# Giving 64 rows of one weight matrix to three of sixteen DMA engines, and moving a small scaling from VectorE to ScalarE

## The chip, the cores and the metric

One core of one Trainium2 chip. The metric is the device time of one launch in microseconds; the kernel before takes 526.28 us (median of three runs, 526.14 to 526.68). The span is the time from the first to the last instruction of a profiled run.

## The reference

One decode step of a transformer block: layer norm of x (4 x 640), attention of 32 heads over a cached window, and a gated feed-forward network, all added up.

```python
xn = layernorm(x)                                   # B=4, D=640
q  = (xn @ wq) ...                                  # 32 heads of 192
k, v = k_cache[:, :, -2048:], v_cache[:, :, -2048:] # 2 x 32 heads x 3 MB, bf16
o  = softmax(q k^T * 192**-0.5) v @ wo
h  = silu(xn @ w1) * (xn @ w3)                      # w1, w3: 640 x 1536
out = x + o + h @ w2                                # w2: 1536 x 640
```

Everything except x is read exactly once, 223 MB in all, and there are only four rows to multiply it with. The kernel is a stream of loads with some arithmetic beside it.

## The kernel before

All large loads are issued by SyncE in one order, and each is split over the 16 DMA engines of the core. K has two buffers, V three, the feed-forward weights one. The program is a list of slots; `add(slot, phase, fn)` puts a step into it.

```python
def load_k(h):
    kt = kpool.tile([P, NJ, Dh], BF16, tag="kt")                      # 2 buffers
    nc.sync.dma_start(out=kt[:]..., in_=k_win[:, h].rearrange("b (p j) d -> p b (j d)", p=PB))
...
xn = const.tile([B, D], BF16, name="xn")
nc.vector.tensor_scalar_mul(out=xn[:], in0=xc[:], scalar1=rstd[:, 0:1])   # line 194
...
def mult(u):                      # VectorE; the last quarter of a head frees its K buffer
    nc.vector.tensor_tensor(out=pr[:], in0=kts[h][:, g * JQ:(g + 1) * JQ, :], in1=qbc[...], op=ALU.mult)
...
def chain_gmax(h):
    ...
    nc.vector.tensor_scalar_mul(out=gneg[:], in0=gmax[:]..., scalar1=-SCALE)   # the softmax shift
...
def ffn_load(name, w, *at):       # w1 in two transfers, w3 in three, over all 128 partitions
    wt = fpool.tile([P, KC, F], BF16, tag="w", name=name)
    for k0, k1 in zip((0,) + at, at + (KC,)):
        nc.sync.dma_start(out=wt[:, k0:k1, :]..., in_=w.rearrange("(p kc) n -> p kc n", kc=KC)[:, k0:k1, :]...)
...
add((h - KBUFS + 1) * GQ, 0, load_k, h)     # K of head h, once head h-2 is multiplied
add(u0 + 2, 0, load_v, h)
add(3, 0, ffn_load, "w1", B_w1, KC // 2)
add(11, 7, ffn_in, "w1")
add(15, 0, ffn_load, "w3", B_w3, KC // 2, KC - 1)
add(NU - 6, 0, load_v, h, 2)                # the last two V tiles, each in two halves
```

Below, K2 is the K load of head 2, and K5 that of head 5.

Of the kernel before, what the change touches and what calls it, by code (L numbers as in the profile page):

```python
# [10 lines left out]
FP32 = mybir.dt.float32  # L11
BF16 = mybir.dt.bfloat16
ALU = mybir.AluOpType
ACTF = mybir.ActivationFunctionType
# [36 lines left out]
def kernel(  # L51
# [19 lines left out]
    nc = tc.nc  # L71
    P = 128
    B, Sq, D = A_x.shape
    _, H, Sk, Dh = A_k_cache.shape
    W = min(4096, max(256, Sk // 4))
    F = B_w1.shape[1]
    KC = D // P
    FC = F // P
    PB = P // B
# [4 lines left out]
    SCALE = float(Dh) ** -0.5  # L84
    EPS = 1e-5
    NG = H // HG
    CT = 32
    QW = HG * Dh
    RPP = QW // P
    NU = H * GQ  # L90
# [12 lines left out]
    fpool = ctx.enter_context(tc.tile_pool(name="ffn", bufs=1))  # L103
    kpool = ctx.enter_context(tc.tile_pool(name="kt", bufs=KBUFS))
    vpool = ctx.enter_context(tc.tile_pool(name="vt", bufs=VBUFS))
    wopool = ctx.enter_context(tc.tile_pool(name="wo", bufs=2))
    const = ctx.enter_context(tc.tile_pool(name="const", bufs=1))
    ppool = ctx.enter_context(tc.tile_pool(name="pr", bufs=PBUFS))
# [4 lines left out]
    ps_t = ctx.enter_context(tc.tile_pool(name="ps_t", bufs=1, space=MemoryType.PSUM))  # L113
# [31 lines left out]
    for k0 in range(0, KC, 2):  # L145
        n = min(2, KC - k0)
        wt = vpool.tile([P, 2, H * Dh], BF16, tag="vt")
        nc.sync.dma_start(out=wt[:, 0:n, :].rearrange("p k n -> p (k n)"),
                          in_=wq_v[:, k0:k0 + n, :].rearrange("p k n -> p (k n)"))
# [4 lines left out]
    idb = const.tile([P, P], BF16, name="idb")  # L154
# [14 lines left out]
    NREP = CT // B  # L169
# [23 lines left out]
    xn = const.tile([B, D], BF16, name="xn")  # L193
# [7 lines left out]
    nc.vector.tensor_copy(out=xnT[:], in_=xnT_ps[:].unsqueeze(2).to_broadcast([P, KC, PB, B]))  # L201


    qbc = const.tile([P, H * Dh], BF16, name="qbc")
    for c0 in range(0, NQ, 6):
        qps = [pool.tile([P, QC], FP32, tag=tag, name="qps")
               for pool, tag in ((ps_add, "ps"), (ps_add, "ps"), (ps_o, "o_ps"), (ps_o, "o_ps"), (ps_m, "mt"), (ps_t, "t"))]
        for kc in range(KC):
            for i, qp in enumerate(qps):
                nc.tensor.matmul(qp[:], lhsT=xnT[:, kc].rearrange("p a b -> p (a b)"),  # L210
                                 rhs=wq_rows[kc][:, (c0 + i) * QC:(c0 + i + 1) * QC],
                                 start=(kc == 0), stop=(kc == KC - 1))
# [62 lines left out]
    def chain_gmax(h):  # L275
        gmax = small.tile([1, B], FP32, tag="gmax")
        nc.vector.tensor_reduce(out=gmax[:], in_=chs[h][1][0:1, 0:P].rearrange("o (p b) -> o b p", b=B),  # L277
                                axis=AX.X, op=ALU.max)
        gneg = small.tile([1, PB, B], FP32, tag="gneg")
        nc.vector.tensor_scalar_mul(out=gneg[:], in0=gmax[:].unsqueeze(1).to_broadcast([1, PB, B]), scalar1=-SCALE)  # L280
        chs[h].append(gneg)

    def chain_bc(h):
# [61 lines left out]
    FW = F // HG  # L345
# [2 lines left out]
    hT = const.tile([P, FC, CT], BF16, name="hT")  # L348
    ffn = {}

    def ffn_load(name, w, *at):
        wt = fpool.tile([P, KC, F], BF16, tag="w", name=name)
        for k0, k1 in zip((0,) + at, at + (KC,)):
            nc.sync.dma_start(out=wt[:, k0:k1, :].rearrange("p k n -> p (k n)"),
                              in_=w.rearrange("(p kc) n -> p kc n", kc=KC)[:, k0:k1, :].rearrange("p k n -> p (k n)"))
        ffn[name] = wt

    def ffn_in(name):
        ffn["ps"] = ps_t.tile([P, FW], FP32, tag="t", name="f_ps")
        for kc in range(KC):  # L360
            for w in range(HG):
                nc.tensor.matmul(ffn["ps"][w * CT:(w + 1) * CT, :], lhsT=xnT[:, kc].rearrange("p a b -> p (a b)")[:, 0:CT],
                                 rhs=ffn[name][:, kc, w * FW:(w + 1) * FW], start=(kc == 0), stop=(kc == KC - 1))

    def ffn_silu():
        nc.scalar.activation(out=sT[:], in_=ffn.pop("ps")[:], func=ACTF.Silu)
# [23 lines left out]
    def add(slot, phase, fn, *args):  # L390
        sched[slot].append((phase, len(sched[slot]), fn, args))
# [4 lines left out]
    for h in range(H):  # L396
        u0, ul = h * GQ, h * GQ + GQ - 1
        if h >= KBUFS:
            add((h - KBUFS + 1) * GQ, 0, load_k, h)
        if h < H - 2:  # L400
            add(u0 + 2, 0, load_v, h)
        for u in range(u0, ul + 1):
            add(u, 1, mult, u)
            add(u + 1, 2, adder, u)
            add(u + 1, 8, reduce_quarter, u)
        add(ul + 1, 9, chain_lmax, h)
        add(ul + 2, 3, chain_tr, h)
        add(ul + 2, 4, chain_gmax, h)
        add(ul + 3, 3, chain_bc, h)
        add(ul + 3, 4, chain_z, h)  # L410
        add(ul + 4, 5, ge_tot, h)
        if h % HG == HG - 1:
            add(ul + 4, 9, ge_rec, h // HG)
        v, m = ends.get(h, (u0 + L, u0 + L + 1))
        add(v, 7, pv, h)
        add(m, 7, ge_sum, h)
        if h % HG == HG - 1:
            add(m + 1, 0, ge_turn, h // HG)
    e = ends[H - 1][1] + 1
    for hg in range(NG - 2):  # L420
        a = ((hg + 1) * HG - 1) * GQ + L + 3
        add(hg * HG * GQ + 8, 0, wo_load, hg)
        add(a, 6, ge_proj, hg, 0, RPP // 2)
        add(a + 1, 6, ge_proj, hg, RPP // 2, RPP)
    add(3, 0, ffn_load, "w1", B_w1, KC // 2)
    add(11, 7, ffn_in, "w1")
    add(11, 9, ffn_silu)
    add(15, 0, ffn_load, "w3", B_w3, KC // 2, KC - 1)
    add(23, 7, ffn_in, "w3")
    add(23, 9, ffn_h)  # L430
    add(16, 6, x_add, 0)
    add(17, 6, x_add, 1)


    for h in range(H - 2, H):
        add(NU - 6, 0, load_v, h, 2)
    add(NU - 6, 0, w2_load, 0)
    add(NU - 6, 0, w2_load, 1)
    add(NU - 6, 0, wo_load, NG - 2)
# [48 lines left out]
```

## Time and profile before

| | before |
|---|---|
| median time | 526.28 us |
| span of the profiled run | 524.4 us |
| loads (queue q1) | 222.96 MB in 12,384 packets, 99.2% of 16 engines' span |
| TensorE, VectorE, ScalarE busy | 68%, 66%, 9% |
| last data packet of the fastest and the slowest DMA engine (from the packets) | 517.8 and 521.05 us |

The page of the kernel before: the busy line, the DMA rows of the slice table (each digit is a tenth, 40 slices), and the queues with packets, MB and share of 16 engines' span.

```profile
PE 357.6 (68%) x2306; PEld 73.9 (14%) x1613; DVE 345.4 (66%) x435; ACT 46.0 (9%) x144; POOL 1.1 (0%) x8
...
DMA  9999999999999999999999999999999999999996
...
q1 hardware_dynamic: 12384, 222.96, 99.2%
q8 instruction: 15, 0.25, 0.2%
q14 instruction: 5, 0.04, 0.0%
```

No compute engine is near its limit (68% at most), and no slice before the last shows the DMA engines under 9 tenths. The two lines of q8 and q14, packets that fetch the program's own instructions while it runs, look negligible. They are not.

The chain of waits of the kernel before, its end: start, duration, what.

```profile
479.99 21.12 DMA vt<-in_A_v_cache_dram
501.12 19.83 DMA w<-in_B_w_dram
520.99 0.75 PE acc L231 x8
521.74 0.47 DVE res L456
```

After the last load landed come 1.2 us of arithmetic and the store of the result; the span is 524.4. So the time is the end of the last load plus 3.4 us.

The trace lists every DMA packet with start, duration and size, but not its engine. The engine can be reconstructed: in steady state a packet starts 3 or 4 ns before another one ends, which I took for the one before it on its engine, and I took every engine to see the transfers in the order of issue. I linked the packets by these two assumptions. For the kernel before this gives 16 sequences of 774 packets with hardly any gap. Where two engines run within a few nanoseconds of each other they can be swapped; the end times are not touched by this. The result, with the packets of 16 KB (q8) and 8 KB (q14) that fall into a gap of a sequence:

```
before: end of last packet (us)   instruction packets in the sequence
517.77 517.83 517.92 518.19 518.19       none
518.34 518.69                            one of 8 KB
519.20                                   one of 16 KB
520.68 520.71 520.76 520.81
520.89 520.91 521.02                     two of 16 KB each
521.05                                   three of 8 KB
```

A 24,576 B packet takes 912 ns. Around a 16 KB packet its engine shows a gap of about 915 ns and one packet that is some 500 ns longer, 1.4 us together; around an 8 KB packet of the last engine 302 + 530 ns. The 16 engines carry the same bytes, but eight of them lose about 3 us to the program's own instructions. Since the kernel waits for the slowest, the others finish early for nothing.

### The profile page before, as it was taken

The page shows a single profiled execution, that of the slowest core. Times are in us where ns is not written, and L with a number is a line of the kernel's source. Part 1 is how long each engine was busy: PE and PEld are TensorE (multiplying, and loading weights), DVE is VectorE, ACT ScalarE, POOL GpSimd, SP SyncE. Part 2 cuts the span into 40 slices and gives each one's busy share as a digit, 9 for nine tenths or more (in the row PEclk, how much of TensorE's full clock was granted, in tenths as well). Part 3 has the DMA queues.
Part 4 walks back from the last instruction along what each step waited for, and adds up shares of the span by engine and source line. Part 5 has one row for each costly group of instructions (what it writes and reads, how often), then busy time and mean ns, then how long its engine had stood idle before and what let it go on. Part 6 is the DMA issues. An engine that isn't in the chain of part 4 may idle for free.

```text
span 524.4 us, 4737 instructions
## 1 busy us (share of the span) xinstructions
PE 357.6 (68%) x2306; PEld 73.9 (14%) x1613; DVE 345.4 (66%) x435; ACT 46.0 (9%) x144; POOL 1.1 (0%) x8
## 2 busy tenths in 40 slices
PE   0965777467758677777668766566676678566884
PEld 0000111111111111111111111111111111111122
DVE  2178756489567767677656876476666867667681
ACT  2111201000000000000000000000000000000011
POOL 0000000000000000000000000000000000000000
PEclk9989887979788987888887998799987988988799
DMA  9999999999999999999999999999999999999996
GB/s 388 422 441 427 431 429 434 427 435 429 435 427 432 434 428 437 427 433 431 433 428 441 423 437 429 433 431 433 426 434 431 434 433 431 431 431 432 425 427 260
DMA packets 12420, 223.26 MB, mean 426 GB/s; under 512 B 1384, under 2 KB 1520, under 8 KB 3440
## 3 DMA queue, kind: packets, MB, share of 16 engines
q1 hardware_dynamic: 12384, 222.96, 99.2%
q8 instruction: 15, 0.25, 0.2%
q14 instruction: 5, 0.04, 0.0%
q10 hardware_dynamic: 16, 0.01, 0.0%
HBM read 222.96 MB, written 0.01 MB: 425 GB/s over the span
## 4 chain that ended last, share of the span: by engine, by line
DMA 64%; DVE 21%; PE 12%; ACT 1%; issue 1%; SPq 0%
DMA kt<-in_A_k_cache_dram 52%; DVE pr L244 15%; PE ps L255 7%; DMA vt<-in_A_v_cache_dram 4%; DMA wt<-in_A_wq_dram 4%; DMA w<-in_B_w_dram 4%; DVE sc L263 3%; PE po L328 3%; PE qps L210 1%; DVE z L299 1%; ACT ex L291 1%; DVE oT L336 1%; PE mt L285 0%; ACT L291 0%; DVE og L333 0%
## 5 line engine op out<-in xcount | busy, mean ns | idle before, releaser
L255 PE MATMUL ps<-pr,idb 128*128 128x512 bf16 x768 | 216.0, 423 | 144.7 <-DVE pr L244 144.7
L244 DVE TENSOR_TENSOR pr<-kt,qbc 128x3072 bf16<-128x3072 bf16 x128 | 223.4, 1746 | 110.2 <-DMA kt<-in_A_k_cache_dram 110.2
L263 DVE TENSOR_REDUCE sc<-ps 128x16 f32<-128x512 f32 x128 | 87.1, 680 | 1.6 <-PE ps L255 1.6
L307 PE MATMUL o_ps<-vt,z 128*8 128x384 bf16 x1024 | 56.8, 362 | 0.2 <-DVE z L299 0.2
L328 PE MATMUL po<-o_sb,sel_w 128*32 128x192 f32 x128 | 49.2, 518 | 0.6 <-ACT o_sb L310 0.6
L307 PEld LDWEIGHTS <-z 128*8 128x8 bf16 x1024 | 25.3, 92 | 93.8 <-issue 83.2
L310 ACT COPY o_sb<-o_ps 128x384 f32<-128x384 f32 x32 | 15.3, 478 | 191.6 <-PE o_ps L307 191.6
L299 DVE TENSOR_TENSOR z<-ex,mask_b 128x256 bf16<-128x256 bf16 x32 | 13.5, 423 | 25.1 <-ACT ex L291 25.1
L288 ACT COPY negm<-mt 128x1 f32<-128x1 f32 x32 | 5.1, 159 | 253.1 <-PE mt L285 253.1
L272 PEld LDWEIGHTS mt<-idf,lmax 128*1 128x1 f32 x32 | 3.3, 104 | 136.6 <-issue 136.6
L328 PEld LDWEIGHTS po<-o_sb,sel_w 128*32 128x32 f32 x128 | 13.9, 131 | 29.6 <-issue 27.0
L255 PEld LDWEIGHTS <-idb 128*128 128x128 bf16 x124 | 11.9, 96 | 39.2 <-issue 32.7
L285 PEld LDWEIGHTS mt<-ones_ff,gneg 1*128 1x128 f32 x64 | 9.4, 182 | 47.0 <-issue 19.6
L210 PE MATMUL qps<-wt,xnT 128*128 128x512 bf16 x59 | 14.9, 410 | 1.3 <-DMA wt<-in_A_wq_dram 0.6
L277 DVE TENSOR_REDUCE gmax<-mt 1x4 f32<-1x128 f32 x32 | 8.8, 275 | 6.3 <-PE mt L272 6.2
L285 PE MATMUL mt<-ones_ff,gneg 1*128 1x1 f32 x64 | 12.1, 256 | 0.6 <-DVE gneg L280 0.6
L216 DVE CAST qbc<-qps 128x512 bf16<-128x512 f32 x6 | 3.8, 684 | 13.0 <-PE qps L210 13.0
L315 PEld LDWEIGHTS po<-rsum,tot_w 128*32 128x32 f32 x64 | 4.4, 108 | 54.1 <-ACT ex L291 27.6
L272 PE MATMUL mt<-idf,lmax 128*1 128x128 f32 x32 | 11.4, 356 | 0.0
L291 ACT ACTIVATE ex<-sc,negm 128x64 bf16<-128x64 f32 x32 | 11.1, 348 | 1.0
L231 PE MATMUL acc<-wo_t,oT 128*4 128x320 bf16 x96 | 9.2, 298 | 2.5 <-DMA wo_t<-in_A_wo_dram 2.5
L199 PE MATMUL xnT_ps<-idb,xn 4*128 4x4 bf16 x5 | 0.4, 178 | 12.6 <-DVE xn L194 12.6
(53 smaller groups left out, 69.1 us busy)
## 6 DMA issues: line engine op xcount, KB each, us to landing
kt<-in_A_k_cache_dram SPq DMA_DIRECT2D x32, 3072.0 KB, 19.4
vt<-in_A_v_cache_dram SPq DMA_DIRECT2D x30, 3072.0 KB, 27.0
wo_t<-in_A_wo_dram SPq DMA_DIRECT2D x8, 960.0 KB, 20.7
wt<-in_A_wq_dram SPq DMA_DIRECT2D x2, 3072.0 KB, 13.3
vt<-in_A_v_cache_dram SPq DMA_DIRECT2D x4, 1536.0 KB, 22.6
w<-in_B_w_dram SPq DMA_DIRECT2D x3, 768.0 KB, 30.4
wt<-in_A_wq_dram SPq DMA_DIRECT2D x1, 1536.0 KB, 19.9
w<-in_B_w_dram SPq DMA_DIRECT2D x2, 640.0 KB, 30.1
```

The lines of the kernel that those rows point to most:

```text
L210: nc.tensor.matmul(qp[:], lhsT=xnT[:, kc].rearrange("p a b -> p (a b)"), rhs=wq_rows[kc][:, (c0 + i) * QC:(c0 + i + 1) * QC], start=(kc == ...
L231: nc.tensor.matmul(acc[i * CT:i * CT + B, :], lhsT=lhsT, rhs=rhs[:, i * N0:(i + 1) * N0], start=first, stop=last)
L244: nc.vector.tensor_tensor(out=pr[:], in0=kts[h][:, g * JQ:(g + 1) * JQ, :], in1=qbc[:, h * Dh:(h + 1) * Dh].unsqueeze(1).to_broadcast([P, ...
L255: nc.tensor.matmul(ps[:], lhsT=idb[:], rhs=pr[:, :, kk * DD:(kk + 1) * DD], start=(kk == 0), stop=(kk == NK - 1))
L263: nc.vector.tensor_reduce(out=scs[h][:, g * JQ:(g + 1) * JQ], in_=pss.pop(u)[:], axis=AX.X, op=ALU.add)
L272: nc.tensor.transpose(out=mt[0:1, 0:P], in_=chs[h][0][:], identity=idf[:])
L285: nc.tensor.matmul(mt[:, P:P + 1], lhsT=gneg[:].rearrange("o p b -> o (p b)"), rhs=ones_ff[:], start=True, stop=True)
L291: nc.scalar.activation(out=ex[:], in_=scs.pop(h)[:], func=ACTF.Exp, bias=negm[:, 0:1], scale=SCALE, accum_out=rsum[:])
L299: nc.vector.tensor_tensor(out=z[:], in0=ex[:].unsqueeze(2).to_broadcast([P, NJ, B]), in1=mask_b[:].unsqueeze(1).to_broadcast([P, NJ, B]), ...
L307: nc.tensor.matmul(o_ps[c * CT:c * CT + 2 * B, :], lhsT=z[:, 2 * jj:2 * jj + 2, :], rhs=vt[:, 2 * jj:2 * jj + 2, :], start=(jj < 4), stop= ...
L310: nc.scalar.copy(out=o_sb[:], in_=o_ps[:])
L328: nc.tensor.matmul(po[sl, 0:Dh], lhsT=sel_w[:, par].rearrange("p a b -> p (a b)"), rhs=o_sb[:, par * Dh:(par + 1) * Dh].rearrange("p (r i) ...
```

## The change

Its intent is to use that spare time: the last 64 rows of w1 (196,608 bytes) go to three engines only, so that the other thirteen carry 12 KB less each. The 64 rows before them go as half rows over all partitions. w3 and the last V tiles are no longer split, w1's product moves from slot 11 to 13, and the scaling of the softmax shift moves from VectorE to ScalarE. Since these rows of w1 now sit on partitions 0–11 and 32–43 alone, x has to be laid out to match, with zeros elsewhere.

```diff
+    KM, PH, LE, LI = KC - 1, P // 2, 3, 4
+    LP, LF, LB = LE * LI, CT + LE * LI, KM * P + PH          # 12, 44, 576
+    xm = ppool.tile([B, 2, PH, 2], BF16, tag="pr", name="xm")
+    nc.gpsimd.memset(xm[:], 0.0)
     ... xe likewise, copies of xn into both, 12 transposes, two copies: xw, xl
-        nc.vector.tensor_scalar_mul(out=gneg[:], in0=gmax[:]..., scalar1=-SCALE)
+        nc.scalar.activation(out=gneg[:], in_=gmax[:]..., func=ACTF.Copy, scale=-SCALE)
+    def w1_load():
+        wt = fpool.tile([P, FH + F], BF16, tag="w", name="w1")
+        we = wopool.tile([LF, 2 * F], BF16, tag="wo", name="w1e")
+        nc.gpsimd.memset(we[:], 0.0)
+        nc.gpsimd.memset(wt[0:LF, FH:], 0.0)
+        nc.sync.dma_start(out=wt[:, 0:FM], in_=w[0:KM * P, :].rearrange("(p kc) n -> p (kc n)", kc=KM))
+        nc.sync.dma_start(out=wt[:, FM:FH], in_=w[KM * P:LB, :].rearrange("r (h n) -> (r h) n", h=2))
+    def w1_low(n):
+        if n < 2:
+            b0 = LB + n * 2 * LP
+            nc.sync.dma_start(out=we[n * CT:n * CT + LP, :],
+                              in_=w[b0:b0 + 2 * LP, :].rearrange("(i e s) n -> e i (s n)", e=LE, s=2))
+        elif n == 2:
+            nc.sync.dma_start(out=wt[0:LP, FH:FH + F], in_=w[LB + 4 * LP:LB + 5 * LP, :].rearrange("(i e) n -> e i n", e=LE))
+        else:
+            nc.sync.dma_start(out=wt[CT:LF, FH:FH + F // LE], in_=w[LB + 5 * LP:D, :].rearrange("i (e n) -> e i n", e=LE))
     ... w1_in: the product over these pieces, 38 matmuls instead of 20
-    add(3, 0, ffn_load, "w1", B_w1, KC // 2)
-    add(11, 7, ffn_in, "w1")
+    add(3, 0, w1_load)
+    for n in range(4):
+        add(4 + 2 * n, 1, w1_low, n)
+    add(13, 7, w1_in)
-    add(15, 0, ffn_load, "w3", B_w3, KC // 2, KC - 1)
+    add(15, 0, w3_load)                                       # one transfer
-        add(NU - 6, 0, load_v, h, 2)
+        add(NU - 6, 0, load_v, h)
```

More of the change, by code (lines that the diff above doesn't have):

```diff
@@ L201 @@
     nc.vector.tensor_copy(out=xnT[:], in_=xnT_ps[:].unsqueeze(2).to_broadcast([P, KC, PB, B]))
+    KM, PH, LE, LI = KC - 1, P // 2, 3, 4
+    LP, LF, LB = LE * LI, CT + LE * LI, KM * P + PH
+    assert D - LB == 5 * LP + LI and F % LE == 0
+    xm = ppool.tile([B, 2, PH, 2], BF16, tag="pr", name="xm")
+    nc.gpsimd.memset(xm[:], 0.0)
+    for i in range(2):
+        nc.vector.tensor_copy(out=xm[:, i, :, i], in_=xn[:, KM * P:LB])
+    xe = ppool.tile([B, 3 + LE, LF], BF16, tag="pr", name="xe")
+    nc.gpsimd.memset(xe[:], 0.0)
+    for g in range(2):
+        b0 = LB + g * 2 * LP
+        nc.vector.tensor_copy(out=xe[:, 0:2, g * CT:g * CT + LP].rearrange("b s (e i) -> b s e i", i=LI),
+                              in_=xn[:, b0:b0 + 2 * LP].rearrange("b (i e s) -> b s e i", e=LE, s=2))
+    nc.vector.tensor_copy(out=xe[:, 2, 0:LP].rearrange("b (e i) -> b e i", i=LI),
+                          in_=xn[:, LB + 4 * LP:LB + 5 * LP].rearrange("b (i e) -> b e i", e=LE))
+    for e in range(LE):
+        nc.vector.tensor_copy(out=xe[:, 3 + e, CT + e * LI:CT + (e + 1) * LI], in_=xn[:, LB + 5 * LP:D])
+    NX = KM + 2
+    xw_ps = ps_t.tile([P, NX + 3 + LE, B], BF16, tag="t", name="xw_ps")
+    for kc in range(KM):
+        nc.tensor.transpose(out=xw_ps[:, kc, :], in_=xn[:, kc:KM * P:KM], identity=idb[0:B, 0:B])
+    for i in range(2):
+        nc.tensor.transpose(out=xw_ps[:, KM + i, :], in_=xm[:, i].rearrange("b r h -> b (r h)"), identity=idb[0:B, 0:B])
+    for i in range(3 + LE):
+        nc.tensor.transpose(out=xw_ps[0:LF, NX + i, :], in_=xe[:, i, :], identity=idb[0:B, 0:B])
+    xw = const.tile([P, NX, NREP, B], BF16, name="xw")
+    nc.vector.tensor_copy(out=xw[:], in_=xw_ps[:, 0:NX, :].unsqueeze(2).to_broadcast([P, NX, NREP, B]))
+    xl = const.tile([LF, 3 + LE, NREP, B], BF16, name="xl")
+    nc.vector.tensor_copy(out=xl[:], in_=xw_ps[0:LF, NX:, :].unsqueeze(2).to_broadcast([LF, 3 + LE, NREP, B]))
     qbc = const.tile([P, H * Dh], BF16, name="qbc")
@@ L279, in chain_gmax @@
         gneg = small.tile([1, PB, B], FP32, tag="gneg")
-        nc.vector.tensor_scalar_mul(out=gneg[:], in0=gmax[:].unsqueeze(1).to_broadcast([1, PB, B]), scalar1=-SCALE)
+        nc.scalar.activation(out=gneg[:], in_=gmax[:].unsqueeze(1).to_broadcast([1, PB, B]), func=ACTF.Copy, scale=-SCALE)
         chs[h].append(gneg)
@@ L349 @@
     ffn = {}
-    def ffn_load(name, w, *at):
-        wt = fpool.tile([P, KC, F], BF16, tag="w", name=name)
-        for k0, k1 in zip((0,) + at, at + (KC,)):
-            nc.sync.dma_start(out=wt[:, k0:k1, :].rearrange("p k n -> p (k n)"),
-                              in_=w.rearrange("(p kc) n -> p kc n", kc=KC)[:, k0:k1, :].rearrange("p k n -> p (k n)"))
-        ffn[name] = wt
-    def ffn_in(name):
+    FM, FH = KM * F, KM * F + F // 2
+    def w1_load():
+        w = B_w1
+        wt = fpool.tile([P, FH + F], BF16, tag="w", name="w1")
[4 more added lines that the diff above has]
+        nc.sync.dma_start(out=wt[:, FM:FH], in_=w[KM * P:LB, :].rearrange("r (h n) -> (r h) n", h=2))
+        ffn["w1"], ffn["w1e"] = wt, we
@@ new lines, in w1_low @@
+    def w1_low(n):
+        w, wt, we = B_w1, ffn["w1"], ffn["w1e"]
+        if n < 2:
[6 more added lines that the diff above has]
+            nc.sync.dma_start(out=wt[CT:LF, FH:FH + F // LE], in_=w[LB + 5 * LP:D, :].rearrange("i (e n) -> e i n", e=LE))
@@ new lines, in w1_in, with mm, main @@
+    def w1_in():
+        wt, we = ffn["w1"], ffn["w1e"]
+        ps = ffn["ps"] = ps_t.tile([P, FW], FP32, tag="t", name="f_ps")
+        def mm(w, lhsT, rhs, c0=0, start=False, stop=False):
+            nc.tensor.matmul(ps[w * CT:(w + 1) * CT, c0:c0 + rhs.shape[1]], lhsT=lhsT.rearrange("p a b -> p (a b)"), rhs=rhs,
+                             start=start, stop=stop)
+        def main(kc):
+            for w in range(HG):
+                mm(w, xw[:, kc], wt[:, kc * F + w * FW:kc * F + (w + 1) * FW], start=(kc == 0), stop=(kc == KM - 1))
+        main(0)
+        for w in range(HG):
+            c0 = FM + (w % 2) * FW
+            mm(w, xw[:, KM + w // 2], wt[:, c0:c0 + FW])
+        for i in range(2):
+            for w in range(HG):
+                mm(w, xl[:, i], we[:, i * F + w * FW:i * F + (w + 1) * FW])
+        for w in range(HG):
+            mm(w, xl[:, 2], wt[0:LF, FH + w * FW:FH + (w + 1) * FW])
+        FE = F // LE
+        for e in range(LE):
+            for w in range(HG):
+                c0, c1 = max(e * FE, w * FW), min((e + 1) * FE, (w + 1) * FW)
+                if c0 < c1:
+                    mm(w, xl[:, 3 + e], wt[0:LF, FH + c0 - e * FE:FH + c1 - e * FE], c0 - w * FW)
+        for kc in range(1, KM):
+            main(kc)
@@ L359, in ffn_in, with w3_load, w3_in @@
+    def w3_load():
+        wt = fpool.tile([P, KC, F], BF16, tag="w", name="w3")
+        nc.sync.dma_start(out=wt[:].rearrange("p k n -> p (k n)"), in_=B_w3.rearrange("(p kc) n -> p (kc n)", kc=KC))
+        ffn["w3"] = wt
+    def w3_in():
         ffn["ps"] = ps_t.tile([P, FW], FP32, tag="t", name="f_ps")
@@ L362, in ffn_in @@
                 nc.tensor.matmul(ffn["ps"][w * CT:(w + 1) * CT, :], lhsT=xnT[:, kc].rearrange("p a b -> p (a b)")[:, 0:CT],
-                                 rhs=ffn[name][:, kc, w * FW:(w + 1) * FW], start=(kc == 0), stop=(kc == KC - 1))
+                                 rhs=ffn["w3"][:, kc, w * FW:(w + 1) * FW], start=(kc == 0), stop=(kc == KC - 1))
     def ffn_silu():
@@ L424 @@
         add(a + 1, 6, ge_proj, hg, RPP // 2, RPP)
-    add(3, 0, ffn_load, "w1", B_w1, KC // 2)
-    add(11, 7, ffn_in, "w1")
-    add(11, 9, ffn_silu)
-    add(15, 0, ffn_load, "w3", B_w3, KC // 2, KC - 1)
-    add(23, 7, ffn_in, "w3")
+    add(3, 0, w1_load)
+    for n in range(4):
+        add(4 + 2 * n, 1, w1_low, n)
+    add(13, 7, w1_in)
+    add(13, 9, ffn_silu)
+    add(15, 0, w3_load)
+    add(23, 7, w3_in)
     add(23, 9, ffn_h)
```

## The prediction

> **What bounds the kernel.** The queue of loads. The slice table shows DMA at 9 tenths in 39 of 40 slices; q1 holds 222.96 MB and 99.2% of 16 engines' span; DVE is 66%, PE 68% busy. The chain of waits is mostly "DMA kt", and ends with DMA w (19.83 us), PE acc 0.75, DVE res 0.47. A 24,576 B packet takes 912 ns, and the next on its engine starts 4 ns before it ends.
>
> The packets can be strung into 16 gapless sequences of 774. All carry the same bytes, but do not end together: by my linking seven end at 517.8–518.7 us, one at 519.2, eight at 520.7–521.05. The difference is instruction fetches on the same engines: each 16 KB packet of q8 costs its engine about 1.4 us (915 ns gap, 500 ns longer neighbour), and fifteen go round eight engines. One further engine has three 8 KB q14 packets, 0.83 us each. The time is the slowest engine's end plus a fixed tail of 3.4 us.
>
> **What the change does.** It balances engines. [...] This trace has no engine numbers, but x_sb's four packets delay four sequences by 48 ns each. Those end at 517.8, 517.9, 518.3 and 521.05 (the last has the three q14 fetches).
>
> Per engine, from packet times less 4 ns:
> - everyone: w1 4.58 to 4.14 us (64 rows fewer), w3 in one transfer instead of three -0.07, last V tiles unsplit -0.07. Sum -0.59 us.
> - three engines: 8 x 6,144 B (230 ns), 4 x 3,072 (117), 4 x 1,024 (about 41, estimated by size), marks: +2.49, net +1.90 us.
>
> If the three are those ending at 517.8–518.3, they end by 520.2 and the others by 520.45: 0.6 us saved. If the one ending at 521.05 is among them, the end moves to 522.9: 1.9 us lost. The awkward three (not four) suggests that it was left out on purpose: 80–85%.
>
> **Off the critical path.** gneg on DVE is 215 ns x 32 (6.9 us) and becomes a ScalarE Copy; neither engine bounds. About 20 more w1 matmuls (before: 40 of 326 ns, overlapping, 20 in 1.3 us). The new transposes and small DVE copies (some 3 us after xn at 12.6) fit before wq lands at 21 us. w1's product moves two slots later and PE waits there for the last small load, behind V2, landing near 77 us (that point was near 76). K5's issue may slip from 82.8 to 84–87 us, but the queue holds work until over 90 us: no idle DMA.
>
> **Predicted time: 525.7 us, range 525.1 to 526.7.** Faster by over 2%: 1%; within 2%: 98%; slower by over 2%: 1%.
>
> **Right or wrong in the profile.** q1 bytes unchanged, DMA still 99%; 48 new packets of 6,144 to 1,024 B; span 0.6 us shorter; the engines' last data packets closer together; K issue times later only around 80 us; gneg's group on ACT.
>
> **What would make it wrong.** The three include the engine with q14 fetches (528.2). More instructions add or shift fetches: PE +60 rows, ACT +32, so a further 8 KB fetch (0.5–0.8 us) on one of the three could eat the gain. PE's wait for w1 starves the queue near 90 us. Run-to-run spread (0.5 us) is as big as the gain.

-0.59 us for every engine puts the slowest at 520.45; +2.49 and -0.59 make the +1.90 of the three, from 517.8–518.3 to 519.7–520.2. The 230 and 117 ns are packets of the trace of before (234 and 121 ns, less 4).

## The result, and the profile after

The changed kernel takes 525.78 us in the median of six runs (525.56 to 526.95), the kernel before 526.38 in six runs of the same rounds. The ratio is 0.9992 with a 95% interval of 0.9979 to 1.0005. A ratio here is the mean time of one kernel's runs over the mean of the other's runs of the same rounds, so it is not quite the ratio of the medians. The difference is the predicted one, but by the times alone it is not clear of noise.

The profiled run took 525.59 us, with a span of 523.8. The same views, after. First the page's busy line, DMA row and queues:

```profile
PE 361.8 (69%) x2336; PEld 75.9 (14%) x1643; DVE 340.9 (65%) x413; ACT 55.8 (11%) x176; POOL 5.6 (1%) x12
...
DMA  9999999999999999999999999999999999999996
...
q1 hardware_dynamic: 11868, 222.96, 99.2%
q8 instruction: 15, 0.25, 0.2%
q14 instruction: 5, 0.04, 0.0%
```

The same bytes in 516 fewer packets. VectorE is 4.5 us less busy, ScalarE 9.8 us more. Then the end of the chain of waits:

```profile
465.17 24.49 DMA vt<-in_A_v_cache_dram
489.68 30.66 DMA w<-in_B_w_dram
520.38 0.76 PE acc L264 x8
521.13 0.47 DVE res L542
```

The arithmetic after the last load is the same 1.2 us and starts 0.6 us earlier (520.38 instead of 520.99). The linked packets show why. The small loads fit only one choice of three among the four sequences that carry x_sb, namely all but the one with three 8 KB packets:

```
after: end of last packet (us)
517.24 517.24 517.49 518.11 518.56        few or no instruction packets, no small loads
519.60 520.19 520.26                      the three with the small loads
519.70 520.02 520.18 520.22
520.22 520.40 520.49                      two of 16 KB each
520.12                                    three of 8 KB
```

(One 16 KB packet near 310 us is split between two sequences by the linking; it belongs to the one with two, so 519.70 and 520.19 are the other way round, as the search named below also has it.) The slowest engine ends at 520.49 instead of 521.05, 0.56 us earlier, where 0.59 was predicted. The three engines went from 517.8–518.3 to 519.6–520.3, just below the others.

These ends contain some chance, since the engines do not finish wq, the first weights, together: they are done with it at 19.9 to 20.7 us before and 19.9 to 20.4 after. Counted from there to its last packet, an engine without instruction packets takes 497.84 us before and 497.22 after, and one with two 16 KB packets 500.68 and 500.05: 0.63 us less each, where 0.59 was predicted. An engine with the small loads and no instruction packet takes 499.73, 1.88 more than before, where 1.90 was predicted. These lengths repeat within 0.02 us in the traces of early_memset and gneg_dve and, for the kernel before, of before_memset. So the gain per engine is far above the noise of the packets, though the times alone do not show it. (A search over the possible links linked all fourteen of them, with the same ends.)

Three places beside that differ. The groups of the scaled shift, before (VectorE) and after (ScalarE): count, busy us and mean ns, idle before.

```profile
L280 DVE TENSOR_SCALAR gneg<-gmax 1x128 f32<-1x128 f32 x32 | 6.9, 215 | 1.1
```

```profile
L313 ACT ACTIVATE gneg<-gmax 1x128 f32<-1x128 f32 x32 | 9.8, 308 | 162.8 <-DVE gmax L310 162.8
```

One scaling is 93 ns longer on ScalarE: 308 ns instead of 215.

The timeline of TensorE after, at w1's product (start, duration; in brackets the idle time and its releaser):

```profile
75.06 0.50 PE L412 MATMUL f_ps<-w1e,xl 44*32 44x384 bf16 x8
80.22 0.83 PE L412 MATMUL f_ps<-w,xl 44*32 44x384 bf16 x10 [4.66 <-DMA w<-in_B_w_dram]
```

TensorE waits 4.7 us for the last small load, which sits behind a whole V tile in the queue. As a result K5 is issued at 90.02 us instead of 82.78.

The timelines of VectorE before and after, at the layer norm's last step:

```profile
12.04 0.54 DVE L194 TENSOR_SCALAR xn<-xc,rstd 4x640 bf16<-4x640 f32 x1
```

```profile
11.35 2.04 DVE L194 TENSOR_SCALAR xn<-xc,rstd 4x640 bf16<-4x640 f32 x1
```

The line is unchanged, but takes 1.5 us longer. The timeline of GpSimd after, in the same stretch:

```profile
9.07 2.65 POOL L390 MEMSET w1e<- 44x3072 bf16 x1
11.67 1.37 POOL L391 MEMSET w<- 44x1536 bf16 x1
```

The two new memsets run without a pause from 9.07 to 13.04 us; VectorE ends xn 0.35 us later, while two tiny VectorE instructions inside the first memset (`vpe` and `rstd`) took the 0.14 and 0.15 us of before. In early_memset, where the two memsets run from 1.81 to 5.77 us, xn takes 0.54 us again. So the memsets stretch xn; by what means, no run shows. The prediction had missed this: it took every unchanged instruction at its old length.

### The profile page after: what moved, and what is told of

It is laid out like the page before. It is cut to its first block, busy times and chain, and to the rows that moved or that the text cites. A ratio compares the mean times of both kernels' runs of the same rounds, so it can differ in the third digit from the quotient of the medians.

```text
span 523.8 us, 4820 instructions
## 1 busy us (share of the span) xinstructions
PE 361.8 (69%) x2336; PEld 75.9 (14%) x1643; DVE 340.9 (65%) x413; ACT 55.8 (11%) x176; POOL 5.6 (1%) x12
## 4 chain that ended last, share of the span: by engine, by line
DMA 60%; PE 20%; DVE 15%; ACT 3%; issue 1%; SPq 1%
DMA kt<-in_A_k_cache_dram 44%; PE ps L288 11%; DMA w<-in_B_w_dram 11%; DVE pr L277 10%; DMA vt<-in_A_v_cache_dram 5%; PE po L361 4%; PE qps L243 3%; DVE sc L296 2%; ACT ex L324 1%; DVE z L332 1%; DMA x_sb<-in_A_x_dram 1%; PE mt L318 1%; ACT L324 0%; ACT negm L321 0%; PE mt L305 0%
## 5 line engine op out<-in xcount | busy, mean ns | idle before, releaser
L340 PE MATMUL o_ps<-vt,z 128*8 128x384 bf16 x1024 | 60.5, 380 | 0.2 <-DVE z L332 0.2
L313 ACT ACTIVATE gneg<-gmax 1x128 f32<-1x128 f32 x32 | 9.8, 308 | 162.8 <-DVE gmax L310 162.8
## 6 DMA issues: line engine op xcount, KB each, us to landing
wo_t<-in_A_wo_dram SPq DMA_DIRECT2D x8, 960.0 KB, 20.7
```

The lines of the kernel that those rows point to most:

```text
L313: nc.scalar.activation(out=gneg[:], in_=gmax[:].unsqueeze(1).to_broadcast([1, PB, B]), func=ACTF.Copy, scale=-SCALE)
L340: nc.tensor.matmul(o_ps[c * CT:c * CT + 2 * B, :], lhsT=z[:, 2 * jj:2 * jj + 2, :], rhs=vt[:, 2 * jj:2 * jj + 2, :], start=(jj < 4), stop= ...
```

## The experiments

Twelve kernels ran. Each call's kernels share the chip and the runs of the kernel before. "End" means the end of the last data packet of the slowest engine in the profiled run. For before, after, a_again, gneg_dve, four_eng, spread16 and v1_first the packets could be linked into engines from beginning to end; for the others only the sorted end times, or parts, are used.

| run | base | runs (us) | median | ratio to before | end | span |
|---|---|---|---|---|---|---|
| a_again | after | 525.68–527.09 | 526.60 | 0.9996 | 521.88 | 525.3 |
| spread16 | after | 526.24–526.83 | 526.42 | 1.0000 | 521.22 | 524.8 |
| gneg_dve | after | 526.01–526.53 | 526.14 | 0.9995 | 520.86 | 524.4 |
| four_eng | after | 527.03–527.23 | 527.19 | 1.0013 | 521.95 | 525.4 |
| early_memset | after | 525.52–525.67 | 525.54 | 0.9984 | 520.40 | 523.8 |
| before_memset | before | 526.38–526.57 | 526.47 | 1.0001 | 521.04 | 524.4 |
| more_pe | early_memset | 526.93–527.26 | 527.15 | 1.0014 | 521.79 | 525.4 |
| dose2 | early_memset | 527.67–528.39 | 528.09 | 1.0031 | 522.78 | 526.4 |
| v1_first | after | 525.56–526.96 | 526.16 | 0.9994 | 521.09 | 524.4 |
| hold_k2 | early_memset | 526.71–527.97 | 527.61 | 1.0025 | 521.57 | 524.9 |
| wrong_ports | early_memset | 527.68–528.08 | 527.99 | 1.0029 | 522.59 | 526.3 |
| own_ports | early_memset | 526.96–527.28 | 527.10 | 1.0014 | 522.08 | 525.4 |

The kernel before had medians of 526.44 (first four), 526.31 (next four) and 526.40 (last four).

### a_again: the changed kernel once more

No edit.

> The changed kernel once more, unedited, to tighten the ratio and to see in a second trace whether the same engines are fast and slow. Balance theory: the three engines that take the small loads end at 519.6 to 520.3 us, the eight with q8 fetches at 520.0 to 520.5, so span about 523.8, about 525.7 us, ratio to before about 0.999. Rival, that the 0.6 us is run-to-run noise: ratio 1.000 and no difference in where the engines' last packets end.

The five runs fell into two groups, 525.68 and 525.78 against 526.60, 527.07 and 527.09. The profile caught one of the slow ones (where this text calls a run of the changed kernel slow, it means 526.6 us or more). The small loads again went to three of the four sequences with x_sb, not to the one with three 8 KB packets. The three ended at 519.66, 519.80 and 520.47, the others at or below 520.52, all as expected, except one: an engine with two 16 KB packets ended at 521.88. Near 46 us, where no instruction packet was recorded, that engine shows this (start ns, duration ns, size, gap ns):

```
45723   65   1536   gap -4
45784    9      4   gap -4
46513 2196  24576   gap 720
48706  912  24576   gap -3
```

It had finished w1's half rows and had nothing to do for 0.72 us; its next packet took 1.28 us longer than usual. That next packet is the first of K2. So one engine ran dry. The timeline of SyncE, K2's issue in the kernel before:

```profile
40.03 0.54 SPq L125 DMA_DIRECT2D kt<-in_A_k_cache_dram  x1
```

in the first profile of the changed kernel:

```profile
41.62 0.54 SPq L125 DMA_DIRECT2D kt<-in_A_k_cache_dram  x1
```

and in this run:

```profile
43.17 0.54 SPq L125 DMA_DIRECT2D kt<-in_A_k_cache_dram  x1
```

From the linked packets, the first engine reached K2's data 6.3 us after its issue in before, 4.2 us in the profiled run of the changed kernel, and 2.7 us here. In all other K loads of before and after it was over 6 us. In this run xn took 2.04 us again. So the change has a second effect that the prediction did not have: it lets the queue come close to empty once, near 46 us.

But the late xn is not what sets this run apart from the faster one, where xn was just as long. K2 came another 1.55 us later because x landed 0.46 us later and TensorE took longer for the q product, in its timeline after and in this run:

```profile
15.15 14.93 PE L243 MATMUL qps<-wt,xnT 128*128 128x512 bf16 x59
```

```profile
15.61 16.16 PE L243 MATMUL qps<-wt,xnT 128*128 128x512 bf16 x59
```

(In the records the first 14 steps between these matmuls, instead of the first 8, take 0.35 to 0.43 us; most later ones take 0.22.) And one step stays open: K2 had been issued 2.6 us before the engine ran dry, while in hold_k2 (below) K2's first packets came 1.3 to 1.7 us after its issue on fifteen engines. Why they came only 3.3 us after it to this engine, no run shows.

### spread16: everything but the imbalance

The last 128 rows of w1 one per partition, over all 16 engines; all other parts of the change kept, except that the memsets fall away with the small loads and w1's product needs 20 matmuls again.

```diff
-        nc.sync.dma_start(out=wt[:, FM:FH], in_=w[KM * P:LB, :].rearrange("r (h n) -> (r h) n", h=2))
-    def w1_low(n): ...
+        nc.sync.dma_start(out=wt[:, FM:], in_=w[KM * P:D, :])
```

> The changed kernel with the last 128 rows of w1 one per partition over all 16 engines; w1 in two transfers, w3 in one, last V unsplit, gneg on ScalarE all kept. Balance theory: all 16 engines carry the same bytes again, slowest end 520.9 us (521.05 less 0.15 for fewer packets), the x_sb engines without fetches back at 517.7 to 518.3; span about 524.25, about 526.2 us, so 0.45 us over the changed kernel. Rival, that the gain is from fewer and larger transfers: as the changed kernel, 523.8 and 525.7. Rival, that PE's wait at 75 to 80 us costs something that hides a larger gain: faster than the changed kernel, since there is no late small load to wait for.

526.42 us, as the kernel before. The linked ends: fifteen engines at or below 520.87 us, where the theory had 520.9, and one at 521.22. The engines with x_sb ended at 517.5, 518.3, 518.4 and, with three 8 KB packets, 520.9. Fewer and larger transfers alone do not give the gain: from the end of wq an engine with two 16 KB packets takes 500.51 us, 0.17 less than before (0.15 expected) and 0.46 more than in the changed kernel. The engines below 518.4 stand idle again. The slowest engine is 0.3 us later than expected, but was late from the start: it was done with wq at 20.71 us, the one that ended at 520.79 at 20.29.

### gneg_dve: the shift scaled by VectorE again

```diff
-        nc.scalar.activation(out=gneg[:], in_=gmax[:]..., func=ACTF.Copy, scale=-SCALE)
+        nc.vector.tensor_scalar_mul(out=gneg[:], in0=gmax[:]..., scalar1=-SCALE)
```

> The changed kernel with the softmax shift scaled by VectorE again, nothing else. Balance theory: off the path, same time within 0.1 us (span 523.8), DVE busy up by about 6.9 us, ACT down by 9.8. Rival, that relieving VectorE is what saved 0.6 us: 0.6 us slower, span 524.4.

The median is 526.14 us, and the lowest run 526.01 against 525.68 of a_again on the same chip. Between the lowest runs lie 0.3 us, neither zero nor 0.6; but a_again's median is 526.60, so the times do not settle it. What the trace shows is not VectorE's time. The page's queue lines of this run:

```profile
q8 instruction: 15, 0.25, 0.2%
q14 instruction: 6, 0.05, 0.0%
```

There are six 8 KB packets instead of five. The sequence that had three now has four, at 47, 201, 356 and 517 us, and ends as the slowest, at 520.86 instead of 520.12. VectorE had executed 52, 178, 310 and 447 instructions (with those of its sequencer) at those times, steps of 126 to 137. The 16,384 B packets come every 258 and 257 of TensorE's instructions in the mean (before and after; weight loads and sequencer counted), about 64 B to each. An estimate from these is 128 instructions to a packet of 8,192 B, which fits VectorE's steps, so I take these packets for VectorE's own instructions. With the shift on ScalarE the program has 422 in all and ends before the fourth packet is fetched. In the kernel before, with 443, the next 8 KB packet was recorded at 526 us, after the end. So the second half of the change, which frees a compute engine that was not the bound, still has an effect: it keeps one instruction packet from the DMA engine that would then be last. From the end of wq that engine takes 500.58 us with four such packets, 499.74 with three (early_memset). How much of these 0.84 us the kernel pays depends on how the other engines started: here the next slowest ended at 520.75, so 0.11 us is what this trace shows. The prediction had put the scaling off the critical path.

### four_eng: four engines instead of three

```diff
-    KM, PH, LE, LI = KC - 1, P // 2, 3, 4
+    KM, PH, LE, LI = KC - 1, P // 2, 4, 4
     ... two loads of 16 partitions and 32 rows each, instead of four loads of 12 partitions
```

> The changed kernel with the last 64 rows over four engines (16 partitions, two loads of 32 rows, 8 packets of 6,144 B each) instead of three. Balance theory: the fourth engine is the one with the three 8 KB q14 fetches, which had no room: it ends at 521.05 - 0.59 + 1.85 = 522.3 us, span about 525.7, about 527.6 us, although each engine gets a quarter less than with three. The other three end at 519.0 to 519.7. Rival, that any few low engines would do and spreading wider is gentler: same as the changed kernel or better (523.8 or less).

527.19 us, all five runs within 0.2 us, and slower than the kernel before. The sequence with three 8 KB packets now takes small loads as well and ends at 521.95 us; the next slowest ends at 520.44. The three others of the small loads end at 519.0, 519.3 and 519.6. The expected end of the fourth was 522.3; its own start was 0.3 us faster than that of before. Three, the awkward number, is right because the fourth engine is the one that fetches VectorE's instructions.

### early_memset: the two memsets where GpSimd is idle

```diff
     make_identity(nc, idf[:])
+    w1_tiles = (fpool.tile([P, F1], BF16, tag="w", name="w1"), wopool.tile([LX, 2 * F], BF16, tag="wo", name="w1e"))
+    nc.gpsimd.memset(w1_tiles[1][:], 0.0)
+    nc.gpsimd.memset(w1_tiles[0][0:LX, F0:], 0.0)
...
-        nc.gpsimd.memset(we[:], 0.0)
-        nc.gpsimd.memset(wt[0:LF, FH:], 0.0)
```

> The changed kernel with the two GpSimd memsets of the w1 tiles moved up to where GpSimd is idle (after the identities, about 2 to 6 us), nothing else. Theory: in the changed kernel they ran beside VectorE's xn (L194), which took 2.04 us instead of 0.54, so the q product and everything to the issue of the third K load came 1.6 us later (41.6 instead of 40.0 us), the queue had only 4.2 us of work left and in some executions one engine ran dry near 46 us and lost 2 us. Then: xn 0.54 us, third K issued at about 40.0, about 5.9 us of queue left, span 523.8 and all five runs at 525.5 to 526.0, none at 526.6 or more. Rival, that the spread of the changed kernel is something else: still some runs of 526.6 to 527.1.

All five runs are between 525.52 and 525.67 us; the ratio to before is 0.9984 with an interval of 0.9971 to 0.9998. The timeline of VectorE:

```profile
11.62 0.54 DVE L198 TENSOR_SCALAR xn<-xc,rstd 4x640 bf16<-4x640 f32 x1
```

and the end of the chain of waits:

```profile
489.61 30.67 DMA w<-in_B_w_dram
520.32 0.76 PE acc L268 x8
521.07 0.47 DVE res L543
```

xn is short again and no run is slow. One number missed. The timeline of SyncE:

```profile
41.21 0.54 SPq L125 DMA_DIRECT2D kt<-in_A_k_cache_dram  x1
```

K2 was expected at 40.0 us. The rest of that delay lies after xn. A part is in the change: from the end of xn to the first matmul of the q product it is 1.76 us instead of 1.00, the new transposes and copies. Another part is not: TensorE was granted 0.68 of its clock between 30 and 36 us in this run, 0.81 in the run of before. That the clock is the cause is an inference from two runs. This is the best of the kernels here, 0.77 us below the median of before.

### before_memset: the memsets alone, in the kernel before

```diff
+    for name in ("xm", "xe"):
+        zx = ppool.tile([B, 256], BF16, tag="pr", name=name)
+        nc.gpsimd.memset(zx[:], 0.0)
+    zt = wopool.tile([CT + 12, 2 * F], BF16, tag="wo", name="zt")
+    nc.gpsimd.memset(zt[:], 0.0)
+    nc.gpsimd.memset(zt[:, 0:F], 0.0)
```

> The kernel before with the same four GpSimd memsets as the changed kernel has at that place (of tiles that nothing reads), nothing else. Theory: xn goes to 2.0 us, the third K load is issued at about 41.6 us instead of 40.0, 4.7 us of queue left instead of 6.3; no engine runs dry in most executions, so the profiled end stays at 521.0 and the span 524.4, and the median within 0.2 us of before, with perhaps one run of five up to 1.4 us longer. Rival, that the memsets cost time in themselves: every run about 1.5 us longer. Rival, that they don't delay xn: 0.54 us as before.

The time is as expected (526.47), but for another reason: xn took 0.71 us, not 2.0. Here the second memset writes the tile of the first and so waits for it, and VectorE got in between. The timeline of VectorE and, below it, of GpSimd:

```profile
11.70 0.71 DVE L194 TENSOR_SCALAR xn<-xc,rstd 4x640 bf16<-4x640 f32 x1
```

```profile
9.41 2.65 POOL L208 MEMSET zt<- 44x3072 bf16 x1
12.12 1.60 POOL L209 MEMSET zt<- 44x1536 bf16 x1
```

xn ended 0.35 us after the first memset, and the second one became longer (1.60 instead of 1.37 us). In four_eng, which has the first memset alone, xn also ended 0.35 us after it and took 0.58 us. It is a useful accident for the question what stretches xn, but no test of what a late xn does to the kernel before.

### more_pe: more instructions for TensorE

```diff
-    nc.at_finalize(keep_loaded_weights)
```

> The kernel with early memsets without the pass that deletes repeated weight loads: some 690 more instructions on TensorE, the same data and products. Fetch theory: q8 packets of 16 KB go from 15 to 17 or 18 [...], the first one or two of the eight engines get a third, and their end moves from 520.2 to about 521.6 us; span about 525.0, about 526.9 us. Rival, that the q8 packets are not what sets the late engines back: 523.8 and 525.7 as without it, TensorE not being the bound.

By the 258 measured in before, 690 instructions are 2.7 packets.

527.15 us, and the end moved from 520.40 to 521.79 us; 521.6 was expected. The page's queue line:

```profile
q8 instruction: 18, 0.29, 0.2%
```

Three more 16 KB packets, no other byte, and 1.4 us: the price of one packet, paid by an engine that now had three. (0.25 us of the longer span is TensorE at the very end.) The count follows TensorE's instructions: 15 packets for 3,958 in before and 4,022 in after, 18 for the 4,714 of this run. TensorE is not the limit here (69% busy in after); the kernel pays these 1.4 us because its limit is the slowest DMA engine.

### dose2: more for the three engines

```diff
+    dm = const.tile([P, 1344], BF16, name="dm")
+    def more_low(n):
+        nc.sync.dma_start(out=dm[n * CT:n * CT + LP, :],
+                          in_=B_w1[n * LP:(n + 1) * LP, 0:1344].rearrange("(i e) n -> e i n", e=LE))
+    for n in range(4):
+        add(40 + 4 * n, 1, more_low, n)
```

> The kernel with early memsets and four more small loads by the same three engines near the middle (12 partitions x 2,688 B each, into a tile that nothing reads): 16 packets of about 103 ns per engine, 1.66 us more on each of the three, nothing on the others. Balance theory: their ends go from 519.6-520.25 to 521.3-521.95 us and they become the bound; span 525.0 to 525.3, about 527.0 us. Rival, that the three still have room: unchanged, 523.8.

The 103 ns of a 2,688 B packet are an estimate by size, from the 117 and 230 ns of 3,072 and 6,144 B in the traces.

528.09 us, end 522.78: slower, as expected, but by 0.8 us too much. The packets show why. During the first two of the four loads (partitions 0–11 and 32–43) no packet of any engine was longer than usual. During the third and fourth (64–75 and 96–107), 23 and 27 packets took up to 1,338 ns instead of 912 on all engines, 0.22 and 0.36 us more per engine. My edit had, without intent, written to partitions on which no small load of the changed kernel writes.

### own_ports: the same dose on partitions 0–11 and 32–43

```diff
-        nc.sync.dma_start(out=dm[n * CT:n * CT + LP, :], ...)          # n = 0..3
+        nc.sync.dma_start(out=dst[(n % 2) * CT:(n % 2) * CT + LP, :], ...)   # n = 0..7, half as wide
```

> The extra small loads again, the same dose (eight loads of 12 partitions x 1,344 B, about 1.7 us on each of the three engines), but all on partitions 0-11 and 32-43. Theory: no packet of another engine gets longer, the three engines end at 521.3 to 522.0 and the others at 520.0 to 520.5; span 525.0 to 525.4, about 527.0 us; less than the 526.4 and 528.1 of the run that used partitions 64-75 and 96-107 for half of the dose. Rival, that the excess of that run was its dose: again 526.4.

527.10 us, end 522.08, at the edge of what was expected. The last three engines end at 521.40, 521.43 and 522.08, all others at or below 520.42. Outside the instruction packets no packet was longer than usual. So the three have no room left for another 1.7 us, and the excess of the run before was the partitions.

### wrong_ports: the changed kernel's small loads on other partitions

```diff
-    LP, LF, LB = LE * LI, CT + LE * LI, KM * P + PH
+    OP = 64
+    LP, LF, LB = LE * LI, OP + CT + LE * LI, KM * P + PH
-            nc.sync.dma_start(out=we[n * CT:n * CT + LP, :],
+            nc.sync.dma_start(out=we[OP + n * CT:OP + n * CT + LP, :],
     ... likewise for the other loads and for xe
```

> The kernel with early memsets with the small loads on partitions 64-75 and 96-107 instead of 0-11 and 32-43, the same rows, bytes and engines. From the two of four extra loads of the run with more small loads that went there: while they last, packets on all 16 engines take 1,000 to 1,300 ns instead of 912. Theory: these loads last 2.5 us in all, so every engine's end moves by some 0.5 to 1.5 us; span 524.3 to 525.3, about 526.0 to 527.1 us. Rival, that partitions do not matter, only which engine: 523.8 and 525.6.

527.99 us, end 522.59: 2.2 us later than with partitions 0–11 and 32–43 (520.40, early_memset), twice what was expected, from the same 192 KB. Added over all packets between 52 and 84 us, each engine lost 2.1 us on average, and single 24,576 B packets took up to 1,744 ns. Even the fastest engine now ends at 519.7 instead of 517.4 (early_memset). So the choice of partitions is worth these 2.2 us. Why these partitions are slower, and how the slowing spreads to all engines, no run shows; the labels own_ports and wrong_ports name my guess at the reason.

### hold_k2: K2 later still

```diff
+    hd = const.tile([P, 640], FP32, name="hd")
+    def hold():
+        for _ in range(4):
+            nc.vector.memset(hd[:], 0.0)
+    add(3, 0.5, hold)
```

> The kernel with early memsets with four VectorE memsets of a scratch tile (about 0.6 us each, 2.5 us) ahead of the product that frees the third K load's buffer, nothing else. Theory: the third K load is issued at 43 to 44 us, with 2 us of queue left, less than the 3.3 us that the last engine's first packet took after its issue in the slow execution: several engines show a gap and one long packet near 46 us, the slowest end moves by 1.3 to 2.5 us, all runs 526.8 to 528.2. Rival, that 2 us of issued-ahead work are enough: 525.6 as without.

The 0.6 us of a memset are an estimate; one of half the size (acc, 128x320) takes 0.33 us in before.

Runs from 526.71 to 527.97 us, the lowest just below the 526.8 expected; it is the profiled one, and its end moved by 1.17 us, where 1.3 to 2.5 was expected. The timeline of SyncE:

```profile
45.02 0.54 SPq L125 DMA_DIRECT2D kt<-in_A_k_cache_dram  x1
```

K2 came even later than meant, and thirteen of the sixteen sequences show a gap near 46.5 us (5.0 us in all; which packet follows which cannot be told there, so single gaps are not known); these and two more show a packet there that is 0.6 to 1.06 us longer than 912 ns; the sixteenth shows an 8 KB instruction packet there. This brings about by intent what one engine showed in a_again: with K2 issued at 45.0 us engines ran dry, and their first packets then took 0.6 to 1.1 us more. It does not show that the issue was too late in a_again itself, where K2 had been issued 2.6 us before the engine ran out; here engines had between 0.8 and 1.5 us.

### v1_first: more queue ahead of K2

```diff
-            add(u0 + 2, 0, load_v, h)
+            add(*((3, 0.5) if h == 1 else (u0 + 2, 0)), load_v, h)
```

> The changed kernel (late memsets kept) with the second V load issued ahead of the third K load instead of after it, nothing else. Theory that the slow executions come from the queue running dry at the third K load: xn still takes 2.0 us and the third K load is still issued at 41 to 43 us, but 7.3 us more of queue lie ahead of it, so no engine runs dry near 46 us: all five runs at 525.5 to 526.0, as with early memsets. Rival, that the late memsets cost something else: some runs of 526.6 to 527.1, as in the changed kernel.

The 7.3 us of a V load are an estimate from the packets: eight of 912 ns, less 4, on each engine.

My expectation failed: 525.56 and 525.58, but also 526.16, 526.20 and 526.96. In the profiled run (526.20) no engine ran dry at K2. Instead it happened at 77.7 us: gaps on four engines, 1.03 us in all, and first packets up to 0.77 us longer. K2 had landed a whole V tile later, so the head's four products and with them the issue of K4 came at 74.2 us instead of 65.6, and the queue ended at about 77.5, 3.2 us or more after K4's issue. The slack was moved, not made. This agrees with the mechanism (an engine without work near the issue of a K load), but it is not the test that I had planned, since memsets and queue order both stay suspects for the run-to-run spread. Nor does it say why 3.2 us did not suffice where hold_k2's first packets took 1.3 to 1.7.

## Why the prediction was right

- **What bounds the kernel**: right. The span is the slowest DMA engine's end plus 3.3 to 3.4 us in before and after.
- **The sum of packet times**: right. Predicted 0.59 us for the slowest engine, measured 0.56; from the end of wq, 0.63 less on engines without small loads and 1.88 more on the three, predicted 0.59 and 1.90. Predicted time 525.7 us, measured 525.78: that this came so close is partly luck, since the next call gave 526.60 for the same kernel and all eleven runs have a median of 525.96. spread16 shows that the imbalance is needed for it, and own_ports that the three engines' room is used up.
- **Which engines**: right, on an assumption that no run had shown before. The three are those without VectorE's instruction packets; four_eng shows the price of taking that one too.
- **Instruction packets as the cause of the skew**: it rested on gaps in one trace, and more_pe made it a shown cause for TensorE's.
- **The shift's scaling**: wrong in part, harmless in its size. Off the critical path as work, but worth one instruction packet, 0.84 us on its DMA engine and 0.11 us of the profiled end (gneg_dve). The prediction had named added fetches as a risk, but those of ScalarE and TensorE.
- **Side effects at the start**: wrong. The prediction said that the new transposes and copies fit before wq lands, and did not cost the memsets. The memsets stretched xn from 0.54 to 2.04 us (a second memset that had to wait for the first left it at 0.71, before_memset), and the transposes and copies put 0.76 us more between xn and the q product. Of eleven runs of the changed kernel, four took 526.6 us or more. The one that was traced lost its time when one engine ran dry at K2; the other three have no trace. With the memsets moved, five of five were fast. Five runs are few for a claim about the share of slow ones: if seven of eleven are not slow, five of five come by chance in one case out of ten, and a_again and early_memset ran on different chips. K2's issue does not separate the kernels well either: 40.9 to 43.2 us in the four traces with a long xn, 39.8 to 41.4 in those with a short one (hold_k2 apart). So the link from the memsets to the dry engine is argued (xn, K2's issue and the gap in one trace; hold_k2 for what a dry engine costs), not shown.
- **TensorE's wait for the last small load**: right in kind, short in size. The load landed at 79.8 us, not at 77, because I read the landing of V2 from its first engine instead of its last; K5 was issued at 90.0, not at 84 to 87. The queue had 6.4 us of work left then (14.1 in before), so it cost nothing.

## What to carry to other kernels

When a kernel is bound by its loads, look at the engines one by one: equal bytes were not equal time here (517.8 to 521.05 us for 774 packets each), and the program's own instructions are traffic (1.4 us of a DMA engine for a 16 KB packet). Filling the spare time of the fast engines paid here with writes on partitions 0–11 and 32–43; on 64–75 and 96–107 the same loads made the end 2.2 us later (wrong_ports), and even on the first set it pays only up to the slowest engine (own_ports). Whatever the change adds at the start of the kernel has to be checked against the first load that waits for a buffer, because there the queue was shortest here: in after 4.2 us of work left when K2 was issued, over 6 us at every other K load.
